# Attention and feed-forward kernel, batches 4 to 7: the logits' maximum by way of DRAM, with the loads of logits, keys and values in other places

## The chip, the cores and the metric

The kernel runs on one core of one Trainium2 chip. The metric is device time in microseconds of one execution, by the median of several. PE is TensorE (matmul), PEld its weight loads, DVE is VectorE, ACT is ScalarE, POOL is GpSimd, and SP is SyncE, which here only issues DMAs. Each engine works through its own instructions in the order in which they were written, and waits on semaphores where an instruction needs another engine's or a DMA's result, or a buffer that is still in use.

## What is computed

```python
def _attn_ref(q, k, v, phi):                      # batch 8, heads 8, seq 576, head_dim 64, n_mem 32
    a = phi - np.max(phi, axis=2, keepdims=True)  # softmax of the logits phi over the 576 rows
    a = np.exp(a)
    a = a / (np.sum(a, axis=2, keepdims=True) + 1e-09)
    k_m = np.einsum('bhsm,bhsd->bhmd', a, k)
    v_m = np.einsum('bhsm,bhsd->bhmd', a, v)
    scores = 1.0 / np.sqrt(q.shape[-1]) * np.matmul(q, k_m.transpose(0, 1, 3, 2))
    ...
    return np.matmul(attn, v_m)                   # attn is the softmax of scores over the 32

def _moe_ref(x, w_in, w_out):                     # x: 4608 tokens of 512, d_ff 2048
    h = x @ w_in
    g = h - np.tanh(h)
    return g @ w_out
```

The attention output of all batches, with heads side by side, is the `x` of the second part.

## The kernel before

**Slots.** The feed-forward part is cut into 18 units of 256 tokens (`u`) and 4 blocks of 512 hidden columns (`fb`). After a start that is written out by hand (`START`), one loop at the end of `split_path` runs over slots with the number 4u + fb. A slot writes its instructions in this order: `mm1` (PE: the hidden pre-activations of `(u, fb)` into the PSUM tile `hs`, from `ph`, `pl`, `ah`, `al`); `g1` (ACT squares, DVE L590); the words of the plan ahead of ";"; ACT's second square (L595); `a_forms` of the slot before (DVE L624, four f16 operations from POOL's result `g` to `f`); `g2` (DVE L600); `mm2_blocks` of two slots earlier (PE L711 and L718, into the PSUM tiles `x`, `o0` and `o1`, and for a unit's last block ACT L756 and L757); the ACT sums of checked weights (L446); the words behind ";"; `g2_high` (ACT L606); `g3` (POOL L611); the late loads; `evict` of a finished unit (DVE L771 to L783 read `x`, `o0` and `o1`, then SP stores); the words behind "|"; and the remaining late words. All slots share one `hs`, one `x`, and one `o0` and `o1`, so the next unit's first products wait for the `evict` of the unit before. In slot 33 the unit `u` = 7 is evicted, and PE's first writes into the new `o0` and `o1` stand in slot 34.

**The plan.** `PLAN` places the attention of batch b in slots relative to the batch's first one, 36 for batch 4, 44 for 5, 52 for 6 and 60 for 7. `FQ` loads the logits by rows (`pt`, 576 KB, in the buffer ring "q" of 2), `FA` the same logits by columns (`e`, one buffer "e"), `X` takes the maximum of each row of `pt` on DVE (`mx`, L149) and spreads it on a diagonal (`dg`, L151), `XP` multiplies `dg` by ones on PE so that every partition has all 256 maxima (`pmx`, L160), `YM` copies them from PSUM (ACT L181) and subtracts them from `e` on POOL (L165, L171), `YE` is the exponential on ACT (L185), `KR` loads keys and values (`kv`, `kt`), and `V` (PE L223, L231) sums keys and values with the weights `e`. Batch 3 has a plan of its own, and batches 0 to 2 lie in the start; for these nothing changes.

**The checked weights.** `PLAN_C` reads each weight block a second time and tests the size of its numbers. `CE` and `CQ` borrow a buffer of "e" or "q" for a block (`chk`, 512 KB); `CW` squares the oldest borrowed block on POOL (L442, `fy`), and ACT sums `fy` in the next slot (L446). `SI` and `NI` use a buffer of "q" for other sums. These words are carried out late in their slot. A load into a buffer waits for the last reader of what lay there before, and SP issues in order, so a load that waits holds up all that stand behind it.

Of the kernel before, what the change touches and what calls it, by code (L numbers as in the profile page):

```python
# [8 lines left out]
F32 = mybir.dt.float32  # L9
# [4 lines left out]
AF = mybir.ActivationFunctionType  # L14
ALU = mybir.AluOpType
# [3 lines left out]
P = 128  # L19
# [20 lines left out]
CW = (  # L40
    0.33333331252017, -0.13333128520786, 0.053934788850892, -0.021660115374759,
    0.0082189218977914, -0.0025104593252184, 0.000420695493864,
)
# [42 lines left out]

class Attention:


    def __init__(self, tc, c, big, ps_a, ins):  # L90
        self.tc, self.c, self.big, self.ps_a, self.ins = tc, c, big, ps_a, ins
# [54 lines left out]
    def top(self, b, d):  # L146
        nc, big = self.tc.nc, self.big
        mx = big.tile([P, 2], F32, tag="mx", name=f"mx{b}")
        nc.vector.tensor_reduce(mx, d["pt"], axis=AX.X, op=ALU.max)  # L149
        dg = big.tile([P, 2, P], F32, tag="kvn", name=f"dg{b}")  # L150
        nc.vector.tensor_tensor(  # L151
            dg, self.c["ident"].unsqueeze(1).to_broadcast((P, 2, P)),
            mx.unsqueeze(2).to_broadcast((P, 2, P)), op=ALU.mult,
        )
        d["dg"] = dg

    def top_all(self, b, d, ps=None):
        nc, dg = self.tc.nc, d["dg"]
        pa = self.psum(f"pmx{b}", ps)
        nc.tensor.matmul(pa[:, 0, 0:256], self.c["ones"], dg.rearrange("p a b -> p (a b)"), start=True, stop=True)  # L160
        d["px"] = pa
# [15 lines left out]

    def expo_pool(self, b, d):

        m = self.big.tile([P, 256], F32, tag="kvn", name=f"ms{b}")  # L180
        self.tc.nc.scalar.activation(m, d["px"][:, 0, 0:256], AF.Copy)  # L181
        self.less_top(self.tc.nc.gpsimd, d["e"], m)

    def expo_exp(self, b, d):
        self.tc.nc.scalar.activation(d["e"], d["e"], AF.Exp)  # L185
# [155 lines left out]
def split_path(ctx, tc, c, ins, out):  # L341
    nc = tc.nc
# [5 lines left out]
    ps_o = ctx.enter_context(tc.tile_pool(name="ps_o", bufs=1, space=PSUM))  # L348
    ps_a = ctx.enter_context(tc.tile_pool(name="ps_a", bufs=1, space=PSUM))
    dram = ctx.enter_context(tc.tile_pool(name="part", bufs=1, space=bass.MemoryType.DRAM))  # L350
# [3 lines left out]
    wout_hi = const.tile([P, 16, DM], F16, name="wout_hi")  # L354
    wout_lo = const.tile([P, 16, DM], F16, name="wout_lo")
    att = Attention(tc, c, big, ps_a, ins)

    RING = {"gg": 3, "h3": 2, "uu": 2, "q": 2, "sc": 2}
    raws = {}
# [131 lines left out]
    st = [dict() for _ in range(B)]  # L491
# [306 lines left out]
    def early(b):  # L798
        return ps_early if b == 0 else None

    def cubic(u, fb, stay):
# [11 lines left out]
        "KA": lambda b: att.load_kv(b, st[b], (0,)), "KB": lambda b: att.load_kv(b, st[b], (1,)), "Q": lambda b, t: att.load_q(b, st[b], t, "q"), "QT": lambda b, t: att.load_q(b, st[b], t, "qt"),  # L813
        "KR": lambda b, r: att.load_kv_half(b, st[b], r),
        "X": lambda b: att.top_bias(b, st[b]) if b < N_ROWS else att.top(b, st[b]), "YX": lambda b: att.expo_rows(b, st[b]),
        "XT": lambda b: att.expo_turn(b, st[b], early(b), ps_o), "XP": lambda b: att.top_all(b, st[b], early(b)),
        "Y": lambda b: att.expo(b, st[b]), "YM": lambda b: att.expo_pool(b, st[b]), "YE": lambda b: att.expo_exp(b, st[b]),
        "V": lambda b, r: att.pool_half(b, st[b], r, st[b]["pk"] if r else None), "N": lambda b, r=None: att.norm(b, st[b]) if r is None else att.norm_half(b, st[b], r),
        "U": lambda b: att.turn(b, st[b], early(b)), "UV": att_turn_v, "W": att_window,
# [24 lines left out]
    for word in START.split():  # L844
        if ":" in word:
            k, tag = word.split(":")
# [3 lines left out]


    PLAN = (
# [9 lines left out]
    )  # L862

    PLAN_C = (
# [229 lines left out]
@with_exitstack  # L1094
def tile_kernel(ctx: ExitStack, tc: tile.TileContext, qt, kva, kvt, pha, phx, w_in, w_out, out):
    nc = tc.nc
    ins = dict(qt=qt, kva=kva, kvt=kvt, pha=pha, phx=phx, w_in=w_in, w_out=w_out)
    const = ctx.enter_context(tc.tile_pool(name="const", bufs=1))
    c = {"first": len(nc.cur_bb.bb.instructions)}
    for name, shape, dt in (  # L1100
        ("ident", [P, P], F32), ("ones", [P, P], F32), ("ones16", [P, 1], F16), ("one", [P, 1], F32),
        ("beta", [P, 1], F32), ("idw", [P, P], F32), ("nidp", [P, P], F16), ("idw", [P, P], F32), ("nid16", [P, P], F16), ("stat", [P, N_CHECK], F32), ("bad", [P, 1], I32),
    ):
        c[name] = const.tile(shape, dt, name=name)
    make_identity(nc, c["ident"])
    nc.vector.tensor_scalar(c["nid16"], c["ident"], -1.0, None, op0=ALU.mult)
    nc.vector.tensor_scalar(c["nidp"], c["ident"], -S_V * S_W / S_P, None, op0=ALU.mult)
    nc.vector.tensor_scalar(c["idw"], c["ident"], S_W, None, op0=ALU.mult)
    nc.gpsimd.memset(c["ones"], 1.0)
    nc.gpsimd.memset(c["ones16"], 1.0)  # L1110
    nc.gpsimd.memset(c["one"], 1.0)
    nc.gpsimd.memset(c["beta"], BETA)
    with ExitStack() as inner:
        split_path(inner, tc, c, ins, out)
    with tc.If(c["wide"] > 0):
        with ExitStack() as inner:
            wide_path(inner, tc, c, ins, out)
# [39 lines left out]
```

## Time and profile before

| | |
|---|---|
| time before, median of 3 runs (lowest, highest) | 656.57 us (656.03, 657.09) |
| the profiled execution: its time, and its span from the first to the last instruction | 656.13 us, 654.2 us |
| granted TensorE clock, mean | 0.999 |
| DVE busy | 522.5 us (80% of the span) |
| ACT busy | 376.1 us (57%) |
| POOL busy | 251.0 us (38%) |
| DMA moved | 84.98 MB, mean 130 GB/s |

The profile is one execution on the chip. Times in its timeline are in microseconds from the span's start. A row gives the start, the duration, the engine, the line of the kernel, the operation, what it writes and reads with its shape, a count, and in brackets the idle time of the engine ahead of it and what ended that. The slots of batch 5 that matter run from about 310 to 345 us on PE, and DVE, ACT and POOL follow some microseconds behind PE.

### The profile page before, as it was taken

How to read it: one execution, taken by the hardware profiler on the slowest of the kernel's cores; microseconds unless marked ns; L12 is line 12 of the kernel's file. 1: busy time of each engine (PE TensorE's matmuls, PEld its weight loads, DVE VectorE, ACT ScalarE, POOL GpSimd, SP SyncE). 2: the span in 40 equal slices, each digit the busy share in tenths (PEclk: the TensorE clock that was granted, in tenths of full speed). 3: DMA queues.
4: the chain of work that ended last, by engine and by line, in shares of the span. 5: the costliest groups of instructions: out<-in, count | busy, mean ns of one | idle time of the engine just before them, and what ended most of it. 6: DMA issues, size and time to landing. Idle time of an engine off the chain costs nothing.

```text
span 654.2 us, 15605 instructions
## 1 busy us (share of the span) xinstructions
PE 638.0 (98%) x6690; PEld 456.1 (70%) x6690; DVE 522.5 (80%) x790; ACT 376.1 (57%) x509; POOL 251.0 (38%) x173
## 2 busy tenths in 40 slices
PE   8779999999999999999999999999999999999996
PEld 4355656566557778777777677877687777887885
DVE  6889999999956687875897779777978686867773
ACT  4477686666423456544655566545655577666541
POOL 0225141222132144451536353624453455455531
PEclk9999999999999999999999999999999999999999
DMA  8999245301423302504350415132433333234201
GB/s 343 393 373 386 99 172 176 124 2 66 146 97 103 134 33 74 176 7 167 101 182 3 169 50 181 55 135 71 147 105 135 102 104 122 64 108 134 86 33 37
DMA packets 26572, 84.98 MB, mean 130 GB/s; under 512 B 2944, under 2 KB 2944, under 8 KB 25728
## 3 DMA queue, kind: packets, MB, share of 16 engines
q1 hardware_dynamic: 25200, 81.55, 36.0%
q10 hardware_dynamic: 1296, 2.36, 1.0%
q8 instruction: 54, 0.88, 0.6%
q14 instruction: 22, 0.18, 0.1%
HBM read 72.37 MB, written 11.53 MB: 128 GB/s over the span
## 4 chain that ended last, share of the span: by engine, by line
PE 78%; DVE 13%; ACT 3%; issue 3%; DMA 1%; POOL 1%; DVEq 0%; ACTq 0%; POOLq 0%
PE hs L575 20%; PE x L718 14%; PE o L711 13%; PE o L718 10%; PE o L654 6%; PE h L575 5%; PE o1h L654 3%; PE pp L527 3%; DVE h L600 2%; DVE h L590 1%; DVE wt L387 1%; PE warm L792 1%; DVE wt L392 1%; DVE ph L545 1%; DVE f L624 1%
## 5 line engine op out<-in xcount | busy, mean ns | idle before, releaser
L611 POOL TENSOR_TENSOR g<-h,g 128x1024 f16<-128x1024 f32 x64 | 138.5, 2165 | 323.9 <-ACT g L606 229.9
L575 PEld LDWEIGHTS <-ph 128*128 128x128 f16 x2304 | 177.0, 98 | 20.5 <-issue 6.0
L575 PE MATMUL hs<-ah,ph 128*128 128x256 f16 (+3 forms) x1152 | 151.5, 246 | 0.0
L590 DVE SCALAR_TENSOR_TENSOR h<-hs,u 128x1024 f32<-128x1024 f32 x54 | 65.8, 1218 | 88.0 <-ACT u L582 88.0
L606 ACT ACTIVATE g<-h 128x1024 f16<-128x1024 f32 x72 | 75.9, 1055 | 92.3 <-DVE h L600 90.2
L575 PE MATMUL hs<-al,ph 128*128 128x256 f16 (+3 forms) x576 | 127.6, 246 | 0.0
L595 ACT ACTIVATE u<-u,beta 128x1024 f32<-128x1024 f32 x72 | 82.4, 1147 | 55.4 <-DVE h L590 54.4
L711 PE MATMUL o<-wout_hi,g 128*128 128x512 f16 x432 | 104.7, 379 | 0.0
L718 PEld LDWEIGHTS <-f 128*128 128x128 f16 x896 | 87.7, 98 | 10.1
L600 DVE SCALAR_TENSOR_TENSOR h<-u,h 128x1024 f32<-128x1024 f32 x72 | 87.4, 1216 | 0.8 <-ACT u L595 0.7
L582 ACT ACTIVATE u<-hs 128x1024 f32<-128x1024 f32 x54 | 55.1, 1019 | 49.6 <-PE hs L575 45.4
L718 PE MATMUL x<-bt,f 128*128 128x256 f16 x672 | 82.5, 273 | 0.0
L718 PEld LDWEIGHTS <-g 128*128 128x128 f16 x672 | 64.4, 98 | 25.8 <-issue 4.3
L711 PEld LDWEIGHTS <-g 128*128 128x128 f16 x432 | 40.5, 98 | 43.9 <-issue 8.1
L624 DVE TENSOR_TENSOR f<-g 128x512 f16<-128x512 f16 x112 | 65.8, 627 | 4.3 <-POOL g L611 3.4
L654 PEld LDWEIGHTS <-g 128*128 128x128 f16 x384 | 36.7, 98 | 46.5 <-issue 3.9
L654 PE MATMUL o<-wout_hi,g 128*128 128x512 f16 x192 | 58.8, 379 | 0.0
L575 PE MATMUL h<-ah,ph 128*128 128x256 f16 (+3 forms) x384 | 49.6, 246 | 0.1
L575 PE MATMUL h<-al,ph 128*128 128x256 f16 (+2 forms) x192 | 42.4, 246 | 0.2 <-POOL al L518 0.2
L545 DVE SCALAR_TENSOR_TENSOR ph<-pp,ph 128x1024 f16<-128x1024 f32 x31 | 37.6, 1212 | 0.6 <-ACT ph L540 0.6
L540 ACT ACTIVATE ph<-pp 128x1024 f16<-128x1024 f32 x32 | 32.6, 1017 | 7.5 <-PE pp L527 7.4
L654 PE MATMUL o<-wout_lo,g 128*128 128x512 f16 x96 | 36.4, 379 | 0.0
(146 smaller groups left out, 974.3 us busy)
## 6 DMA issues: line engine op xcount, KB each, us to landing
q<-in_qt_dram SPq DMA_DIRECT2D x16, 576.0 KB, 4.9
kv<-in_kva_dram SPq DMA_DIRECT2D x16, 516.0 KB, 4.7
chk<-in_w_in_dram SPq DMA_DIRECT2D x16, 512.0 KB, 5.7
chk<-in_w_out_dram SPq DMA_DIRECT2D x16, 512.0 KB, 3.3
out_dram<-r SPq DMA_DIRECT2D x27, 256.0 KB, 2.4
kv<-in_kva_dram SPq DMA_DIRECT2D x6, 1032.0 KB, 8.7
raws<-in_w_in_dram SPq DMA_DIRECT2D x12, 512.0 KB, 7.0
raw<-in_w_out_dram SPq DMA_DIRECT2D x12, 512.0 KB, 7.2
```

Source lines behind the costliest of these rows:

```text
L545: nc.vector.scalar_tensor_tensor(pl, pa, S_P / (S_V * S_W), ph, op0=ALU.mult, op1=ALU.subtract)
L575: nc.tensor.matmul(hp[:, k, tu : tu + w], px[:, g, cs], d[ax][:, g, ta : ta + w], start=(n == 0), stop=(n == 5),)
L582: nc.scalar.activation(uu, hp, AF.Square, scale=1.0 / (S_A * S_P))
L590: nc.vector.scalar_tensor_tensor(h3, hp, C2 * S_G / (S_A * S_P), uu, op0=ALU.mult, op1=ALU.mult)
L595: nc.scalar.activation(uu, uu, AF.Square, bias=c["beta"])
L600: nc.vector.scalar_tensor_tensor(h3, uu, CC, hp, op0=ALU.add, op1=ALU.mult)
L606: nc.scalar.activation(gg[:, 0], h3, AF.Copy)
L611: eng.tensor_tensor(gg[:, 1], h3, gg[:, 0], op=ALU.subtract)
L624: nc.vector.tensor_tensor(o, x, y, op=op)
L654: nc.tensor.matmul(o, gx[:, k, P * tt : P * tt + P], wx[:, 4 * fb + k, :], start=(first and k == 0 and wx is wout_hi and gx is gh), stop=( ...
L711: nc.tensor.matmul(o[th], gg[:, 0, k, P * th : P * th + P], wout_hi[:, 4 * fb + k, :], start=(first and k == 0), stop=False)
L718: nc.tensor.matmul(dst, a(1 - n, kk), b(n, kk), start=(new and kk == 0 and n == 0), stop=(end and kk == 1 and n == 1))
```

## The change

For batches 4 to 7 the diagonal, the matmul with ones and ACT's copy are dropped. DVE's row maxima (`mx`, 128 x 2 numbers) are written to a small DRAM tile by a DMA on SP, and a second DMA on SP, written a slot later (`XL`), reads that tile into every partition (`ms`, 128 x 256). POOL subtracts from this tile, whose two maxima of a partition now lie side by side, so it is read with a step of two. `FQ` moves from slot -11 to -12, `X` from -10 to -11, and `KR` from -10 to -9; `FA`, `YM`, `YE` and `V` keep their slots. In `PLAN_C`, `CQ` and `CE` change places in slots 21, 30, 38 and 46, so that the first block to be checked, and so the first buffer to be freed, is one of "q".

```diff
@@ top
         nc.vector.tensor_reduce(mx, d["pt"], axis=AX.X, op=ALU.max)
+        if b > 3 and self.dram:
+            d["mx"] = self.dram.tile([P, 2], F32, tag=f"mx{b}", name=f"mxd{b}")
+            nc.sync.dma_start(d["mx"], mx)
+            return
         dg = big.tile([P, 2, P], F32, tag="kvn", name=f"dg{b}")
...
+    def load_top(self, b, d):
+        d["ms"] = self.big.tile([P, P, 2], F32, tag="kvn", name=f"ms{b}")
+        self.tc.nc.sync.dma_start(d["ms"], d["mx"].unsqueeze(0).to_broadcast((P, P, 2)))
@@ expo_pool
-        m = self.big.tile([P, 256], F32, tag="kvn", name=f"ms{b}")
-        self.tc.nc.scalar.activation(m, d["px"][:, 0, 0:256], AF.Copy)
-        self.less_top(self.tc.nc.gpsimd, d["e"], m)
+        m, e, eng = d["ms"].rearrange("p x r -> p r x"), d["e"], self.tc.nc.gpsimd
+        eng.tensor_tensor(
+            e[:, 0:8].rearrange("p (c r) x -> p c r x", r=2), e[:, 0:8].rearrange("p (c r) x -> p c r x", r=2),
+            m.unsqueeze(1).to_broadcast((P, 4, 2, P)), op=ALU.subtract,
+        )
+        for r in range(2):
+            rs = slice(64 * r, 64 * r + 64)
+            eng.tensor_tensor(e[rs, 8], e[rs, 8], m[rs, r], op=ALU.subtract)
@@ split_path
+    att.dram = dram
...
+        "XL": lambda b: att.load_top(b, st[b]),
@@ PLAN
-        (-11, "FQ{0} FA{0}"), (-10, "; X{0} KR{0}0 KR{0}1"), (-9, "| XP{0} YM{0}"), (-8, "; YE{0}"), ...
+        (-12, "FQ{0}"), (-11, "FA{0} ; X{0}"), (-10, "; XL{0}"), (-9, "KR{0}0 KR{0}1 | YM{0}"), (-8, "; YE{0}"), ...
@@ PLAN_C
-        (21, "; CE CQ CQ"), (22, "CW"), (23, "CW"), (24, "CW"), (30, "CE CQ"), (31, "CW CE SI0"), (32, "CW CW ; SS0"),
-        (38, "CE CQ"), (39, "CW CE SI1"), (40, "CW CW ; SS1"), (46, "CE CQ"), (47, "CW CE SI2"), (48, "CW CW ; SS2"),
+        (21, "; CQ CQ CE"), (22, "CW"), (23, "CW"), (24, "CW"), (30, "CQ CE"), (31, "CW CE SI0"), (32, "CW CW ; SS0"),
+        (38, "CQ CE"), (39, "CW CE SI1"), (40, "CW CW ; SS1"), (46, "CQ CE"), (47, "CW CE SI2"), (48, "CW CW ; SS2"),
```

**DVE in slot 33** (the first is `g2` of unit 8, block 1; the `r` rows are the eviction of unit 7, and the two with `o700` and `o701` free `o0` and `o1`). Before:

```order
L600 SCALAR_TENSOR_TENSOR h381_4164<-u81_4162,h381_4164 128x1024
L771 SCALAR_TENSOR_TENSOR r70_4183<-x_2448,r70_4183 128x256
L772 SCALAR_TENSOR_TENSOR r71_4184<-x_2448,r70_4183 128x256
L773 TENSOR_TENSOR r70_4183<-r70_4183,r71_4184 128x256
L776 TENSOR_TENSOR r71_4184<-r71_4184 128x256
L783 SCALAR_TENSOR_TENSOR r70_4183<-o700_3885,r70_4183 128x512
L783 SCALAR_TENSOR_TENSOR r71_4184<-o701_3886,r71_4184 128x512
```

And now, with the lines of the changed file (L771 is L787, L773 is L789, L783 is L799):

```order
L616 SCALAR_TENSOR_TENSOR h381_4164<-u81_4162,h381_4164 128x1024
L151 TENSOR_REDUCE mx5_4223<-pt5_4077 128x2
L787 SCALAR_TENSOR_TENSOR r70_4181<-x_2448,r70_4181 128x256
L788 SCALAR_TENSOR_TENSOR r71_4182<-x_2448,r70_4181 128x256
L789 TENSOR_TENSOR r70_4181<-r70_4181,r71_4182 128x256
L792 TENSOR_TENSOR r71_4182<-r71_4182 128x256
L799 SCALAR_TENSOR_TENSOR r70_4181<-o700_3883,r70_4181 128x512
L799 SCALAR_TENSOR_TENSOR r71_4182<-o701_3884,r71_4182 128x512
```

The maximum `mx5` now stands ahead of the eviction; it stood a slot later, with `dg5`, behind `g2` and the transpose `af4`, and both are gone from there.

**SP in slots 30 to 34** (the `chk` rows are borrowed weight blocks, `q41` queries of batch 4, `pt5` and `e5` the logits of batch 5, `r70` and `r71` the stores of unit 7). Before:

```order
L369 DMA chk3_3930<-in_w_in_dram 128x512
L369 DMA chk4_3932<-in_w_in_dram 128x512
L137 DMA q41_3984<-in_qt_dram 128x1152
L369 DMA chk5_4034<-in_w_in_dram 128x512
L102 DMA pt5_4166<-in_phx_dram 128x1152
L106 DMA e5_4168<-in_pha_dram 128x1152
L784 DMA out_0_dram<-r70_4183 128x512
L784 DMA out_0_dram<-r71_4184 128x512
L128 DMA kv500_4343<-in_kva_dram 128x1032
```

And now:

```order
L385 DMA chk3_3928<-in_w_in_dram 128x512
L385 DMA chk4_3930<-in_w_in_dram 128x512
L139 DMA q41_3982<-in_qt_dram 128x1152
L385 DMA chk5_4032<-in_w_in_dram 128x512
L104 DMA pt5_4077<-in_phx_dram 128x1152
L108 DMA e5_4166<-in_pha_dram 128x1152
L154 DMA mxd5_4225<-mx5_4223 128x2
L800 DMA out_0_dram<-r70_4181 128x512
L800 DMA out_0_dram<-r71_4182 128x512
L165 DMA ms5_4341<-mxd5_4225 128x256
L130 DMA kv500_4406<-in_kva_dram 128x1032
```

The order of the first six is the same, but not their buffers: `chk3` and `chk5` had the one buffer "e" and `chk4` one of "q", while now `chk3` has "q" and `chk4` and `chk5` have "e". So `chk5` waited for POOL's square of `chk3`, and now waits for that of `chk4`. `pt5` waited for POOL's square of `chk4`; it needs only that of `chk3` now, but stands behind `chk5` in the queue. POOL's order is unchanged: in slot 32 the squares of `chk4` and `chk5` follow each other directly, then the product with `sz40`, then `g81` of slot 33. The two new DMAs stand between `e5` and the keys and values. Batches 6 and 7 have the same rows in slots 38 to 42 and 46 to 50; for batch 4 the logits are loaded in slot 24, when the borrowed blocks of slot 21 have one buffer each and none waits for another.

More of the change, by code (lines that the diff above doesn't have):

```diff
@@ L87 @@
 class Attention:
+    dram = None
     def __init__(self, tc, c, big, ps_a, ins):
@@ L815, in split_path @@
         "X": lambda b: att.top_bias(b, st[b]) if b < N_ROWS else att.top(b, st[b]), "YX": lambda b: att.expo_rows(b, st[b]),
-        "XT": lambda b: att.expo_turn(b, st[b], early(b), ps_o), "XP": lambda b: att.top_all(b, st[b], early(b)),
+        "XT": lambda b: att.expo_turn(b, st[b], early(b), ps_o), "XP": lambda b: att.top_all(b, st[b], early(b)), "XL": lambda b: att.load_top(b, st[b]),
         "Y": lambda b: att.expo(b, st[b]), "YM": lambda b: att.expo_pool(b, st[b]), "YE": lambda b: att.expo_exp(b, st[b]),
```

2 rows, old and new, of the table PLAN are left out of this document.

## The prediction

> **What bounds the kernel now.** I read the span first, then the busy times over the long middle part, then the timeline of one slot at a time.
>
> ```profile
> span 654.2 us, 15605 instructions
> ```
> ```profile
> 192.00:624.00 432.00, 431.46 (x4733) 330.88 (x4731) 335.20 (x512) 251.42 (x340) 192.91 (x125) 1.00 0.32 105
> ```
>
> The second row gives the stretch, its length, and the busy time of PE, PEld, DVE, ACT and POOL. From 192 to 624 us PE has no work for only 0.54 us. So whatever PE no longer issues there is won, nearly in full, and whatever PE must wait for is lost in full: there is no later idle time in which to get it back. The question is which instructions PE loses, and which waits come near enough to hold it.
>
> **What PE loses.** One matmul of 256 columns in two passes, before the first `hs` of slots 28, 36, 44 and 52:
>
> ```profile
> 341.31 0.27 PE L718 MATMUL o<-wout_lo,f 128*128 128x256 f16 x1
> 341.42 0.60 PE L160 MATMUL pmx<-dg,ones 128*128 128x256 f32 x2
> 341.86 0.27 PE L575 MATMUL hs<-ah,ph 128*128 128x256 f16 x1
> ```
> ```profile
> 350.03 0.27 PE L718 MATMUL o<-wout_lo,f 128*128 128x256 f16 x1
> 350.14 0.27 PE L575 MATMUL hs<-ah,ph 128*128 128x256 f16 x1
> ```
>
> With it, `hs` starts 0.55 us behind the last L718; without it 0.11 us. So it costs 0.44 us of PE, and four times that is **-1.76 us**. `dg` on DVE and the copy on ACT go too, but PE doesn't wait for them, so I cost them at nothing.
>
> **What moves ahead of the eviction.** PE's first matmul into the new `o0` waits for the first L783, which reads the old one. These are the rows of slot 33 on DVE, and the matmul on PE:
>
> ```profile
> 325.43 1.22 DVE L600 SCALAR_TENSOR_TENSOR h<-u,h 128x1024 f32<-128x1024 f32 x1
> 326.56 0.42 DVE L771 SCALAR_TENSOR_TENSOR r<-x,r 128x256 f32<-128x256 f32 x1
> 327.01 0.42 DVE L772 SCALAR_TENSOR_TENSOR r<-x,r 128x256 f32<-128x256 f32 x1
> 327.36 0.41 DVE L773 TENSOR_TENSOR r<-r,r 128x256 f32<-128x256 f32 x1
> 327.69 0.42 DVE L776 TENSOR_TENSOR r<-r 128x256 f32<-128x256 f32 x1
> 328.02 0.68 DVE L783 SCALAR_TENSOR_TENSOR r<-o,r 128x512 f32<-128x512 f32 x1
> ```
> ```profile
> 330.10 0.38 PE L711 MATMUL o<-wout_hi,g 128*128 128x512 f16 x1
> ```
>
> The first L783 ends at 328.70, so there are 1.40 us to spare. The maximum now stands between L600 and L771:
>
> ```profile
> L149 DVE TENSOR_REDUCE mx<-pt x6: 1309/1312/1343, 82.1 to 471.1; 128x2 f32<-128x1152 f32 x6
> ```
>
> It takes 1.31 us, about 1.35 us from its start to the next one's. By itself that would just fit. Two things come on top.
>
> *First, the logits arrive too late for it.* In batches 5 to 7 the load of `pt` stands behind that of `chk5`, which now waits until POOL has squared `chk4`, as `pt` itself did before:
>
> ```profile
> 321.10 2.04 POOL L442 TENSOR_TENSOR fy<-chk 128x512 f32<-128x512 f32 x2
> 323.10 1.33 POOL L318 TENSOR_TENSOR sc<-sc,sz 128x576 f32<-128x576 f32 x1
> 327.81 2.29 POOL L611 TENSOR_TENSOR g<-h,g 128x1024 f16<-128x1024 f32 x1 [3.38 <-ACT g L606]
> ```
> ```profile
> 322.17 0.33 SPq L102 DMA_DIRECT2D pt<-in_phx_dram  x1
> ```
>
> The first square ends at about 322.1 and `pt` is issued at 322.17. So `FQ`, a slot earlier in the plan, is in fact issued no earlier: `chk5` goes at 322.17 and `pt` some 0.4 us behind it. For two such loads in a row there is a pair of before:
>
> ```profile
> 249.51 0.34 SPq L102 DMA_DIRECT2D pt<-in_phx_dram  x1
> 249.90 0.42 SPq L106 DMA_DIRECT2D e<-in_pha_dram  x1
> ```
> ```profile
> pt<-in_phx_dram SPq DMA_DIRECT2D x1, 576.0 KB, 3.8
> e<-in_pha_dram SPq DMA_DIRECT2D x1, 576.0 KB, 4.8
> ```
> ```profile
> chk<-in_w_in_dram SPq DMA_DIRECT2D x1, 512.0 KB, 3.7
> ```
>
> The last number is from issue to landing. The second of a pair lands 0.39 + 4.8 = 5.2 us after the first's issue; the first one here is 64 KB smaller, so I take 5.1. `chk5` lands at 322.17 + 3.7 = 325.9 and `pt` at 327.3. DVE, free at 326.56, waits 0.75 us. Then the maximum, and L771 starts at about 328.7, L772 at 329.1, and L773 would at 329.5.
>
> *Second, POOL holds L773 up.* L773 reads two SBUF tiles. The same kind and size of operation, `dg`, shows what that means while POOL works:
>
> ```profile
> 335.33 2.14 POOL L611 TENSOR_TENSOR g<-h,g 128x1024 f16<-128x1024 f32 x1 [5.22 <-ACT g L606]
> ```
> ```profile
> 336.12 1.63 DVE L151 TENSOR_TENSOR dg<-ident,mx 128x256 f32<-128x256 f32 x1
> ```
>
> POOL's instruction ended at 337.47 and `dg` at 337.75: 1.63 us instead of the 0.41 of L773. Before, L773 and L776 were just ahead of POOL's `g` of 327.81. Where is that `g` now? POOL squares `chk5` when it lands, 326.0 to 327.0; ACT's sum of that square and its `g` follow:
>
> ```profile
> 324.88 0.71 ACT L446 ACTIVATE fy<-fy,one 128x512 f32<-128x512 f32 x1
> 325.49 0.19 ACT L446 ACTIVATION_READ_ACCUMULATOR fy<-fy,one 128x1 f32 x1
> 326.68 1.06 ACT L606 ACTIVATE g<-h 128x1024 f16<-128x1024 f32 x1 [1.00 <-DVE h L600]
> ```
>
> So the sum starts at 327.1, ACT's `g` at 327.85, and POOL's `g` runs from 328.95 for 2.13 us, to 331.1. L773, ready at 329.5, waits for its end. By the `dg` row the next instruction starts about 0.2 us behind that end; L776 takes 0.33, L783 0.69. The first L783 ends at 332.3, and PE, ready at 330.10, goes on at 332.37: **2.27 us lost** in each of batches 5, 6 and 7, +6.8 us. What else is late there catches up in PE's wait: the next `g1`, which frees `hs`, ends near 334.0, and PE needs `hs` at 333.14 + 2.27 = 335.4. ACT's `g` and POOL's are some 2 to 4 us late in slot 34, but DVE then saves the maximum and `dg`, 3 us.
>
> [...]
>
> *Batch 4* has its logits early, but the same order in slot 25:
>
> ```profile
> 260.52 0.42 DVE L771 SCALAR_TENSOR_TENSOR r<-x,r 128x256 f32<-128x256 f32 x1
> ```
> ```profile
> 261.83 2.24 POOL L611 TENSOR_TENSOR g<-h,g 128x1024 f16<-128x1024 f32 x1 [3.77 <-issue]
> ```
> ```profile
> 264.81 0.38 PE L711 MATMUL o<-wout_hi,g 128*128 128x512 f16 x1
> ```
>
> L771 moves to 261.87 and L773 to 262.67, into `g`, which ends at 263.9. Then 0.2 + 0.33 + 0.69: the first L783 ends at 265.15, and PE waits until 265.2, **0.4 us**.
>
> **What I cost at nothing.** The two new DMAs have no row. `mx` is written from about 328.7, and behind the two stores, which SP holds until 332.9, `ms` is issued near 333.4. With each at a landing between 0 and the 3.7 us of a 512 KB load, `ms` is there by 337.1, and POOL asks for it ten microseconds later:
>
> ```profile
> 347.04 2.37 POOL L165 TENSOR_TENSOR e<-e,ms 128x1024 f32<-128x1024 f32 x1
> ```
> ```profile
> 357.63 0.32 PE L223 MATMUL pkv<-kv,e 128*32 128x129 f32 x4
> ```
>
> Keys and values are issued behind `ms`, from about 333.8 to 336, over 20 us ahead of `V`; four of the six went out only after the old maximum before, so they are hardly later.
>
> POOL's subtraction now reads `m` with a step of two numbers. From below: the 2.37 us stay, as only the step of one input changes. From above, the dearest two-input row of POOL per element:
>
> ```profile
> L171 POOL TENSOR_TENSOR e<-e,ms x8: 522/582/650, 282.1 to 486.5; 64x128 f32<-64x128 f32 x8
> ```
> ```profile
> 352.50 1.06 ACT L606 ACTIVATE g<-h 128x1024 f16<-128x1024 f32 x1 [0.71 <-DVE h L600]
> ```
>
> 582 ns for 128 is 4.5 ns an element, 4.7 us for 1024, 2.3 us more. ACT's exponential would pass that on, less the 0.71 us that it then idles: up to 1.6 us a batch, 6.4 in all, if it reached PE. I take nothing, since most of those 582 ns look like a fixed part.
>
> [...]
>
> **The sum**: -1.76 + 3 x 2.27 + 0.4 = +5.45 us. The profiled execution took 656.13 us, of which the span is 654.2; it becomes 661.6. It lay 0.44 us under the median, so against that the forecast is **662.0 us**.
>
> **The rivals.**
> - *All is hidden*: the logits land in time, and POOL's `g` does not meet L773. Only PE's matmuls count: 656.57 - 1.76 = 654.8 us, **faster**. It decides at 1.40 us: if the maximum delays the eviction by less, PE never waits. For it, 1.35 us alone would fit; against it, `pt` is issued no earlier than before.
> - *Late logits, but no lock*: L783 ends at 327.3 + 0.05 + 1.35 + 1.46 + 0.69 = 330.85, a loss of 0.8 us in three batches, none in batch 4: 656.57 + 2.4 - 1.76 = 657.2 us, **no change**. It would need `pt` within 0.5 us of `chk5`, or `g` later than I have it.
> - *Lock, but logits in time*, because the wait of `chk5` is shorter than I read it. POOL's `g` ends at 329.9, L783 at 331.1: 1.1 us in three batches: 656.57 + 3.3 + 0.4 - 1.76 = 658.5 us, slower.
> - *The strided subtraction reaches PE too*: up to 662.0 + 6.4 = 668.4 us, slower.
> - *The change doesn't do what it says*, in that the logits have no lead: this is part of the forecast.
>
> **How the numbers follow.** The forecast has 0.52, all hidden 0.16, late logits without the lock 0.14, the lock alone 0.10, the subtraction 0.08. A measurement of this kernel can tell about 0.2%, 1.3 us, from no change. So faster has 0.16, the same 0.14, slower 0.70. The range from 655.9 to 666.5 us leaves out the hidden case, and of the last one what lies above two thirds of its price (662.0 + 4.5).
>
> **What would show it.** In the changed profile `pt` of batch 5 should be issued some 0.4 us behind `chk5`, with POOL idle for 3 to 4 us between two squares; `mx` should wait for the DMA; L773 (now L789) should last over 1.5 us instead of 0.41 in four evictions; and PE should wait for L783 (now L799) three times for about 2.3 us and once for 0.4. If L789 keeps 0.41 us, the lock is wrong here; if PE waits for nothing, the hidden rival is right; if PE's new waits stand at `V` or at `hs`, I have missed a path.

## The result, and the profile after

| | before | after |
|---|---|---|
| median (lowest to highest, runs) | 656.31 us (656.03 to 657.09, 4) | 665.75 us (664.84 to 666.26, 4) |
| after against before, 95% interval | | 1.0139 [1.0127, 1.0151] |
| profiled execution, its span | 656.13 us, 654.2 us | 666.26 us, 664.5 us |

The change costs 9.4 us, 8.3 to 9.9 us by the interval. The forecast was 5.45 us over the median of before as it then stood, 656.57 us: the sign was right, the size too small. These are the rows of the changed kernel that answer to the first two of before, the span and the busy times of PE, PEld, DVE, ACT and POOL over the middle part:

```profile
span 664.5 us, 15593 instructions
```
```profile
192.00:634.00 442.00, 432.06 (x4730) 330.33 (x4729) 335.15 (x508) 248.90 (x336) 191.75 (x125) 1.00 0.31 104
```

PE's work is nearly the same, but the part is 10 us longer: PE has 9.94 us without work where it had 0.54. The list of PE's waits (sum, times, longest) names them, with the one line that the list of before had of the same kind below it:

```profile
PE x L734 <- DVE r L788: 4.7, 3, 1.8
...
PE o L727 <- DVE r L799: 2.4, 4, 0.8
PE pp L543 <- DVE kvn L254: 2.4, 3, 0.9
```
```profile
PE pp L527 <- DVE kvn L239: 0.2, 1, 0.2
```

The first two are the eviction, the third is a wait that was not in the forecast. To see what each costs I compare where PE starts the first `hs` of a slot. From slot 34 to 35 before, and after:

```profile
324.86 0.27 PE L575 MATMUL hs<-ah,ph 128*128 128x256 f16 x1
...
333.14 0.27 PE L575 MATMUL hs<-ah,ph 128*128 128x256 f16 x1
```
```profile
326.82 0.27 PE L591 MATMUL hs<-ah,ph 128*128 128x256 f16 x1
...
337.52 0.27 PE L591 MATMUL hs<-ah,ph 128*128 128x256 f16 x1
```

8.28 us became 10.70: the eviction of unit 7 costs 2.42 us. The same subtraction for every slot gives this ledger (us, against before):

| slots | what | forecast | measured |
|---|---|---|---|
| 26 to 29 | batch 4 in all, its matmul included | 0.4 - 0.44 | +0.49 |
| 34 to 35, 42 to 43, 50 to 51 | eviction | 3 x 2.27 | +2.42, +2.33, +2.74 |
| 35 to 36, 43 to 44, 51 to 52 | the matmul of ones gone | 3 x -0.44 | -0.44, -0.44, -0.43 |
| 38 to 39, 46 to 47, 54 to 55 | `pp` waits for `kvn` | 0 | +0.73, +0.70, +0.68 |
| 18 to 71 | all (the rest is -0.04) | +5.45 | +8.74 |

Ahead of slot 18, where both kernels have the same code, this execution was 1.47 us later (193.55 us instead of 192.08). In the 14 profiles of this study that point lies between 191.60 and 194.07 us, so I count that as variation of the start. All comparisons of slots below are taken from slot 18 on.

**The eviction** went as the prediction has it. SP, DVE and POOL in slot 33:

```profile
324.12 0.33 SPq L385 DMA_DIRECT2D chk<-in_w_in_dram  x1
324.54 0.38 SPq L104 DMA_DIRECT2D pt<-in_phx_dram  x1
```
```profile
329.58 1.35 DVE L151 TENSOR_REDUCE mx<-pt 128x2 f32<-128x1152 f32 x1 [2.48 <-DMA pt<-in_phx_dram]
330.85 0.41 DVE L787 SCALAR_TENSOR_TENSOR r<-x,r 128x256 f32<-128x256 f32 x1
331.29 0.42 DVE L788 SCALAR_TENSOR_TENSOR r<-x,r 128x256 f32<-128x256 f32 x1
331.64 1.86 DVE L789 TENSOR_TENSOR r<-r,r 128x256 f32<-128x256 f32 x1
```
```profile
328.18 1.04 POOL L458 TENSOR_TENSOR fy<-chk 128x512 f32<-128x512 f32 x1 [4.08 <-DMA chk<-in_w_in_dram]
329.18 1.16 POOL L333 TENSOR_TENSOR sc<-sc,sz 128x576 f32<-128x576 f32 x1
331.09 2.12 POOL L627 TENSOR_TENSOR g<-h,g 128x1024 f16<-128x1024 f32 x1 [0.76 <-ACT g L622]
```

`pt` is issued 0.42 us behind `chk5`, not earlier; `mx` waits 2.48 us for it; POOL waits 4.08 us for `chk5`, ACT's sum of that block and its own `g` come late with it, and so POOL's `g` starts at 331.09 and ends at 333.21; L789, which took 0.41 us in the kernel before (there L773), takes 1.86 and ends at 333.50, 0.29 us behind that `g`. This is what the forecasts and I call the lock: L789 reads two SBUF tiles, comes up while POOL's `g` is under way, and ends only behind it. PE waits twice:

```profile
331.87 0.27 PE L734 MATMUL x<-wout_hi,g 128*128 128x256 f16 x1 [1.49 <-DVE r L788]
...
334.49 1.89 PE L727 MATMUL o<-wout_hi,g 128*128 128x512 f16 x8 [0.72 <-DVE r L799]
```

The first matmul into `x`, ahead of those into `o0`, already waits for L788, the last reader of `x`. Only the remaining 0.72 us is waited for where I had put all of it.

**The new wait**, five slots on. PE before and after, and what DVE and POOL of the changed kernel do in slot 36:

```profile
362.92 0.41 PE L527 MATMUL pp<-win_hi,vh 64*32 64x512 f16 x8 [0.20 <-DVE kvn L239]
```
```profile
367.60 0.41 PE L543 MATMUL pp<-win_hi,vh 64*32 64x512 f16 x8 [0.93 <-DVE kvn L254]
```
```profile
352.01 2.94 DVE L640 TENSOR_TENSOR f<-g 128x512 f16<-128x512 f16 x2
```
```profile
351.67 2.40 POOL L191 TENSOR_TENSOR e<-e,ms 128x1024 f32<-128x1024 f32 x1
```

Where POOL does not hold them, the two f16 operations of `f` take 0.75 us together (at 324.43 us in the same profile, while POOL waits for `chk5`); here POOL's subtraction is under way when the first begins, and they take 2.94: the first lasts 2.34, to 354.35, 0.28 us behind the end of the subtraction at 354.07. Before, `f` came 1.02 us behind the start of that subtraction and took 2.21 (at 348.06 and 347.04 us); now it comes 0.34 us behind it. Counted from the first `hs` of slot 36 it is the subtraction that has moved, from 5.18 us to 5.86; `f` begins at 6.21 us in both kernels, and in both its first operation ends behind the subtraction. DVE leaves slot 36 later, and `kvn`, which frees the PSUM tile that `pp` needs, is late.

**Batch 4**, in slots 25 to 28, is a small copy of both: L789 lasts 1.67 us, PE waits for L799, and in slot 27, where `hs` needs a `ph` that DVE made late (L561), it waits again and gives back most of what the matmul had saved:

```profile
264.04 1.67 DVE L789 TENSOR_TENSOR r<-r,r 128x256 f32<-128x256 f32 x1
```
```profile
266.70 1.89 PE L727 MATMUL o<-wout_hi,g 128*128 128x512 f16 x8 [0.26 <-DVE r L799]
...
270.68 0.23 PE L591 MATMUL hs<-ah,ph 128*128 128x64 f16 x2 [0.23 <-DVE ph L561]
```

### The profile page after: what moved, and what is told of

Read it like the earlier page. It is cut to its first block, busy times and chain, and to the rows that moved or that the text cites. A ratio compares the mean times of both kernels' runs of the same rounds, so it can differ in the third digit from the quotient of the medians.

```text
span 664.5 us, 15593 instructions
## 1 busy us (share of the span) xinstructions
PE 640.2 (96%) x6682; PEld 455.3 (69%) x6682; DVE 523.9 (79%) x786; ACT 373.7 (56%) x505; POOL 250.1 (38%) x173
## 4 chain that ended last, share of the span: by engine, by line
PE 57%; DVE 20%; issue 8%; DMA 5%; ACT 5%; POOL 3%; SPq 0%; DVEq 0%; ACTq 0%; POOLq 0%
PE hs L591 14%; PE o L727 9%; PE x L734 8%; PE o L734 7%; PE o L670 6%; PE h L591 4%; DVE f L640 4%; PE o1h L670 3%; DVE h L616 3%; DVE h L606 3%; DMA pt<-in_phx_dram 2%; ACT u L598 2%; PE pp L543 2%; POOL g L627 2%; DMA raw<-in_w_out_dram 2%
## 5 line engine op out<-in xcount | busy, mean ns | idle before, releaser
L616 DVE SCALAR_TENSOR_TENSOR h<-u,h 128x1024 f32<-128x1024 f32 x72 | 87.4, 1216 | 0.8 <-ACT u L611 0.7
L561 DVE SCALAR_TENSOR_TENSOR ph<-pp,ph 128x1024 f16<-128x1024 f32 x31 | 37.6, 1214 | 2.6 <-ACT ph L556 2.6
L458 POOL TENSOR_TENSOR fy<-chk 128x512 f32<-128x512 f32 x32 | 33.7, 1062 | 12.5 <-DMA chk<-in_w_in_dram 12.5
```

Source lines behind the costliest of these rows:

```text
L561: nc.vector.scalar_tensor_tensor(pl, pa, S_P / (S_V * S_W), ph, op0=ALU.mult, op1=ALU.subtract)
L616: nc.vector.scalar_tensor_tensor(h3, uu, CC, hp, op0=ALU.add, op1=ALU.mult)
```

## The experiments

Times are medians; ratios are against the kernel before on the same chip, with 95% intervals. "Stalls" are the steps of the ledger: the three evictions, and the three steps of `kvn`.

| run | time, us | ratio | batch 4 | evictions | `kvn` |
|---|---|---|---|---|---|
| the changed kernel | 665.75 | 1.0139 [1.0127, 1.0151] | +0.49 | 2.42, 2.33, 2.74 | 0.73, 0.70, 0.68 |
| e1 maximum behind the eviction | 655.88 | 0.9990 [0.9979, 1.0001] | -0.43 | 0, 0.01, 0 | 0.40, 0.39, 0.43 |
| e2 logits ahead of the block | 666.02 | 1.0132 [1.0115, 1.0149] | +0.51 | 0.22, 0.41, 0.14 | 0.75, 0.76, 0.71 |
| e3 blocks as before | 661.55 | 1.0072 [1.0057, 1.0088] | +0.51 | 1.12, 1.10, 1.11 | 0.74, 0.73, 0.69 |
| e4 DRAM path alone | 655.99 | 0.9997 [0.9985, 1.0010] | -0.43 | 0, 0, 0 | 0.28, 0.24, 0.24 |
| e5 logits in a place of their own | 656.11 | 0.9998 [0.9988, 1.0007] | +0.49 | 0, 0.01, 0 | 0.26, 0.26, 0.27 |
| e6 e1, subtraction on DVE | 656.57 | 1.0007 [0.9994, 1.0019] | -0.43 | 0, 0, 0 | 0.59, 0.42, 0.83 |
| e7 changed kernel, subtraction on DVE | 666.41 | 1.0153 [1.0138, 1.0168] | +0.50 | 3.11, 2.46, 2.65 | 0.90, 0.88, 0.86 |
| e8 e5, subtraction on DVE | 657.14 | 1.0010 [1.0001, 1.0020] | +0.48 | 0, 0, 0 | 0.43, 0.41, 0.40 |
| e9 e6, small parts first | 654.45 | 0.9965 [0.9954, 0.9977] | -0.43 | 0, 0.01, 0 | -0.27, -0.12, -0.13 |
| e10 changed kernel, no subtraction | 664.00 | 1.0110 [1.0095, 1.0125] | +0.47 | 2.70, 2.39, 2.80 | -0.26, -0.11, -0.13 |
| e11 e7, small parts first | 663.64 | 1.0108 [1.0092, 1.0125] | +0.49 | 2.58, 2.40, 2.45 | -0.27, -0.11, -0.13 |
| e12 changed kernel, eviction from PSUM | 667.87 | 1.0170 [1.0157, 1.0184] | -0.03 | 3.88, 3.71, 4.12 | 0.26, 0.24, 0.22 |

**e1: the maximum behind the eviction.**

```diff
-(-11, "FA{0} ; X{0}")
+(-11, "FA{0} | X{0}")
```

> The changed kernel with the maximum behind the eviction instead of ahead of it; the load of the logits still waits behind the borrowed block, and POOL still waits for that block. Theory A (the eviction is held: late logits, then the maximum, then POOL's lock on the eviction's two-input sum): the three waits of PE for the eviction are gone, and with the backlog the wait at kvn; 656.3 - 1.8 = 654.5 us, at most 655.5. Rival B (POOL's wait for the block and ACT's late g are what costs, wherever the maximum stands): PE still waits some 2 us in each of three batches, about 662 us. Rival C (the DRAM path itself, its DMAs or the strided subtraction, costs): above 656.3 us, with waits of PE at V or of POOL for ms.

655.88 us. The eviction no longer waits for the logits and nothing of its stall is left, though POOL still waits 4.05 us for `chk5` and ACT 2.56 us for its square. So the maximum ahead of the eviction is needed for the loss, and the waits of POOL and ACT cost nothing at the eviction by themselves. The time is 0.4 us above the range of theory A: a price is paid elsewhere, 0.4 us a batch at `kvn`.

**e2: the logits ahead of the block, by the plan.**

```diff
-(-12, "FQ{0}"), ... (31, "CW CE SI0"), ... (39, "CW CE SI1"), ... (47, "CW CE SI2")
+(-13, "| FQ{0}"), ... (31, "CW SI0 CE"), ... (39, "CW SI1 CE"), ... (47, "CW SI2 CE")
```

> The changed kernel with the logits' load issued a slot earlier still, ahead of the borrowed block that waits; the maximum stays ahead of the eviction, and POOL still waits for the block. Theory A: logits in time, DVE takes the maximum at once and is through the eviction's two-input sums before POOL's g, or waits for POOL's shorter product only; PE waits for the eviction by less than 0.5 us, total 654.5 to 656.5 us. Rival B: POOL and ACT are as late as in the changed kernel, so about 662 us or more.

666.02 us, far outside. The eviction stall nearly went, but the edit made a new wait: with the logits loaded first, the queries of `SI0` got the buffer of `chk3`, and ACT, which squares them, and then PE, waited. ACT's and PE's waits:

```profile
ACT sqi L466 <- POOL fy L458: 9.7, 3, 3.2
```
```profile
PE pni L480 <- ACT g L622: 4.9, 3, 1.6
```

With PE held ahead of the eviction by this new wait, the run can't say what the late logits cost; e5 moves them without that change of buffers.

**e3: the blocks in the order of before**, with all else as changed.

```diff
-(21, "; CQ CQ CE"), ... (30, "CQ CE"), ... (38, "CQ CE"), ... (46, "CQ CE")
+(21, "; CE CQ CQ"), ... (30, "CE CQ"), ... (38, "CE CQ"), ... (46, "CE CQ")
```

> The changed kernel with the borrowed blocks in the order of before, so that no block waits ahead of the logits and POOL has no wait; the logits land just in time, and the maximum stays ahead of the eviction. Theory A with the lock: the two-input sum runs into POOL's g and takes over 1.5 us, PE waits about 1.1 us in three batches and 0.4 in the first; 658 to 659 us. Without a lock: the maximum alone delays the eviction by 1.35 us, PE waits 0.4 us at x; about 656 us. Rival B: nothing waits, 654.6 us.

661.55 us. `mx` follows L616 without a wait, and yet L789 meets POOL's `g`:

```profile
324.02 2.25 DVE L640 TENSOR_TENSOR f<-g 128x512 f16<-128x512 f16 x2
...
330.17 1.61 DVE L789 TENSOR_TENSOR r<-r,r 128x256 f32<-128x256 f32 x1
```
```profile
329.37 2.14 POOL L627 TENSOR_TENSOR g<-h,g 128x1024 f16<-128x1024 f32 x1 [3.38 <-ACT g L622]
```

The eviction loses 1.1 us a batch, the price that the rival "lock, but logits in time" gave. `kvn` loses as much as in the changed kernel, 2.2 us, which puts the time above the 658 to 659 us expected; so this part of the loss does not depend on the order of the blocks.

**e4: the DRAM path alone**, every word in its slot of before.

```diff
-(-12, "FQ{0}"), (-11, "FA{0} ; X{0}"), (-10, "; XL{0}"), (-9, "KR{0}0 KR{0}1 | YM{0}")
+(-11, "FQ{0} FA{0}"), (-10, "; X{0} XL{0} KR{0}0 KR{0}1"), (-9, "| YM{0}")
```

(and `PLAN_C` as in e3)

> The kernel before with the path through DRAM alone: loads and maximum in the slots of before, the maximum written to DRAM and read into all partitions right behind it, borrowed blocks in the order of before. Theory A: only PE's four matmuls are gone and nothing else is late; 654.6 us, PE without new waits, POOL not waiting for ms. Rival C: above 656.3 us, with POOL's subtraction later or longer, and PE waiting at V or at kvn.

655.99 us: nothing is lost by the two DMAs or by the subtraction with a step of two. All four matmuls are won, 1.74 us by the ledger, and 0.76 of it goes back at `kvn`: PE arrives there 0.44 us sooner, and DVE does not. The median is 1.4 us above the 654.6 expected. By the ledger 1.0 us is won from slot 18 on; the ratio shows less of it, and in the profiled execution slot 18 itself began 1.02 us later than before, which lies within the variation of the start.

**e5: the late logits by themselves.** A word `LQ` loads `pt` late in slots 31, 39 and 47, ahead of `chk5`'s load; every buffer is that of the changed kernel.

```diff
-(-12, "FQ{0}"),
-(31, "CW CE SI0"), ... (39, "CW CE SI1"), ... (47, "CW CE SI2")
+(24, "FQ4 CW"), ...
+(31, "CW SI0 LQ5 CE"), ... (39, "CW SI1 LQ6 CE"), ... (47, "CW SI2 LQ7 CE")
```

> The changed kernel, but in batches 5 to 7 the load of pt stands ahead of chk5's in SP's queue (issued late in slot 31, behind the queries q41 and ahead of the block that waits for a square), so that it waits only for the square of the first block. Nothing else is moved: the maximum still stands ahead of the eviction and the buffers are those of the changed kernel. Theory A (late logits carry L789 into POOL's g): pt is issued near 315 us, mx starts directly behind L616 instead of waiting 2.48 us for the DMA, L789 then ends before POOL's g begins and takes about 0.4 us, and the eviction stall of PE falls from 2.3 to 2.7 us to under 0.4 in batches 5 to 7; the wait for kvn (0.7 us a batch) stays or halves: 656 to 658.5 us. Rival B (the lock does the harm by itself, with logits in time as well, as in the run with the blocks in the order of before): 1.1 us a batch are left and kvn stays: 660.5 to 662.5 us. Rival C (the place of the maximum ahead of the eviction does it, whatever the logits and POOL do): no change against the changed kernel, 665 to 666 us.

656.11 us, as theory A has it. `pt` goes out 8 us ahead of `chk5`, `mx` does not wait, and the eviction passes ahead of `g`:

```profile
314.88 0.33 SPq L104 DMA_DIRECT2D pt<-in_phx_dram  x1
323.25 0.33 SPq L385 DMA_DIRECT2D chk<-in_w_in_dram  x1
```
```profile
323.55 0.75 DVE L640 TENSOR_TENSOR f<-g 128x512 f16<-128x512 f16 x2
...
326.14 1.34 DVE L151 TENSOR_REDUCE mx<-pt 128x2 f32<-128x1152 f32 x1
...
328.19 1.09 DVE L789 TENSOR_TENSOR r<-r,r 128x256 f32<-128x256 f32 x1
```
```profile
327.85 1.16 POOL L333 TENSOR_TENSOR sc<-sc,sz 128x576 f32<-128x576 f32 x1
329.76 2.14 POOL L627 TENSOR_TENSOR g<-h,g 128x1024 f16<-128x1024 f32 x1 [0.76 <-ACT g L622]
```

L789 took 1.09 us, not the 0.4 expected: it met POOL's shorter product with `sz`, until 329.01, and that still fits into the slack. So 1.35 us of maximum do fit ahead of the eviction here, as the rival "all is hidden" said; in the changed kernel, late logits carried it into `g`.

That it fits has a reason which no forecast named. While POOL waits for `chk5` it does not hold DVE's `f`, which takes 0.75 us here and 2.25 in e3, beside POOL's second square and its product. So DVE comes to the maximum 7.69 us behind the first `hs` of slot 33 here, and 9.21 us behind it in e3. There, with POOL's work in its place of before, the same maximum costs 1.1 us although the logits are in time.

**e6 and e7: the subtraction on DVE**, on top of e1, and on the changed kernel.

```diff
 def expo_pool
-... self.tc.nc.gpsimd
+... self.tc.nc.vector
```

> The kernel with the maximum behind the eviction (655.88 us), and in addition the subtraction L191 and its two small parts L197 on DVE instead of POOL, in the same place of the order. Theory A (POOL's subtraction locks out DVE's f in slot 36, 2.6 us instead of 0.75, and so makes kvn late): the subtraction takes about 1.1 us and the two small parts 0.2 each on DVE, in the 2.16 us that DVE idles ahead of L606 of slot 36; f takes 0.75; PE's wait for kvn (1.5 us in 3) goes: 654.0 to 655.2 us. Rival B (kvn is late through DVE's own backlog, and the added 1.5 us on DVE make it later): 656 to 658 us, with f at 0.75 and the wait for kvn no smaller. Rival C (the maximum arrives too late for DVE, which then waits at the subtraction for ms, landing near 341 us): idle time of DVE ahead of L191, and PE waits for hs instead: 656 to 659 us.

> The changed kernel as it is, but for the subtraction on DVE. Theory A: the eviction stall of PE (2.3 to 2.7 us a batch) stays, since nothing is altered ahead of slot 35, and only the wait for kvn (0.73, 0.70 and 0.69 us) goes: 663.3 to 664.3 us. Rival B (the wait for kvn is the eviction's delay come again, not the subtraction): 665 to 667 us.

656.57 and 666.41 us: both lie in the ranges of rival B, and the wait for `kvn` grew, as it said. `f` has its 0.75 us in e6, but now DVE's own small parts run into POOL's `g`. DVE and POOL of e6:

```profile
344.67 1.21 DVE L191 TENSOR_TENSOR e<-e,ms 128x1024 f32<-128x1024 f32 x1
345.81 3.38 DVE L197 TENSOR_TENSOR e<-e,ms 64x128 f32<-64x128 f32 x2
```
```profile
345.31 2.57 POOL L627 TENSOR_TENSOR g<-h,g 128x1024 f16<-128x1024 f32 x1 [4.02 <-issue]
347.84 1.20 POOL L320 TENSOR_TENSOR sc<-sc,sm 128x576 f32<-128x576 f32 x1
```

The two small parts took 3.38 us, until 349.19: they were done behind `g` (to 347.88) and POOL's next operation (to 349.04). They were expected at 0.2 us each. DVE lost as much time to POOL as before, in another place, so these runs fit rival B, but do not exclude theory A. **e8**, e5 with the same edit, has the same flaw:

> The changed kernel with both: the load of pt ahead of chk5's, and the subtraction on DVE. If the two terms are separate, the two gains add up: by theory A of both, nothing is left of the changed kernel's loss and the four matmuls' 1.7 us are won, 654.3 to 655.8 us. If instead one of them only moves the loss on to the other place, it ends no lower than the better of the two alone plus 1 us.

657.14 us, 1 us above e5 alone: the loss only moved, as the second forecast has it.

**e9 to e11: DVE's loss taken away.** In e9 (on e6) and e11 (on e7) the two small parts stand ahead of the large one:

```diff
+for r in range(2): ... eng.tensor_tensor(e[rs, 8], e[rs, 8], m[rs, r], op=ALU.subtract)
 eng.tensor_tensor(e[:, 0:8] ..., m ..., op=ALU.subtract)
-for r in range(2): ... eng.tensor_tensor(e[rs, 8], e[rs, 8], m[rs, r], op=ALU.subtract)
```

In e10 the changed kernel has none of the three lines.

> The kernel with the maximum behind the eviction and the subtraction on DVE, with the two small parts L197 (64x128) ahead of the large one L191 instead of behind it. In the run before, the second small part met POOL's g and lasted until its end: the two took 3.38 us. Theory A (what makes kvn late is the time that DVE loses to POOL's lock in slots 35 and 36, wherever it is lost): the small parts take about 0.2 us each and L191 1.2, they end ahead of L606's wait for ACT's u, POOL's g starts some 0.8 us later instead; f of slot 36 keeps 0.75; DVE leaves slot 36 1.5 us or more earlier and PE's wait for kvn (2.1 us in 3) goes or falls under 0.6: 654.2 to 655.3 us. Rival B (kvn waits for something else, pkv or PE's own order): the wait stays at 1.5 to 2.1 us, 655.7 to 656.7 us.

> The changed kernel without the subtraction of the maximum from e in batches 4 to 7 (L191 and L197 left out; the maximum is still made, written and read back). Theory A (the wait for kvn comes from the lock between POOL's subtraction and DVE's f in slot 36, 2.94 us there): f takes 0.75, PE's wait for kvn (0.73, 0.70, 0.69 us) is gone, the eviction stall stays: 663.2 to 664.2 us. Rival B (the eviction's lateness alone makes kvn late): 665 to 666.3 us with the wait still there.

> The changed kernel with the subtraction on DVE, small parts first. Theory A as for the kernel without a subtraction, but with 1.5 us more of DVE's time in slot 35, of which 1.84 us are idle there: 663.3 to 664.5 us, with PE's wait for kvn under 0.2 us a batch. Rival B: 665 to 666.5 us.

654.45, 664.00 and 663.64 us; all three times as theory A has them. In the two on the changed kernel the eviction stalls stay, and the steps of `kvn` go from +0.7 to below zero. DVE in e9, slot 35 and the `f` of slot 36, and POOL:

```profile
342.64 0.57 DVE L193 TENSOR_TENSOR e<-e,ms 64x128 f32<-64x128 f32 x2
343.23 1.23 DVE L194 TENSOR_TENSOR e<-e,ms 128x1024 f32<-128x1024 f32 x1
...
347.16 1.02 DVE L640 TENSOR_TENSOR f<-g 128x512 f16<-128x512 f16 x2
```
```profile
343.28 3.17 POOL L627 TENSOR_TENSOR g<-h,g 128x1024 f16<-128x1024 f32 x1 [4.02 <-issue]
```

Now DVE has the large subtraction under way when `g` comes up at 343.28, 0.05 us later, and POOL is the one that is held: `g` takes 3.17 instead of 2.13 us, and nobody waits for it. `f` takes 1.02 us, not quite the 0.75 expected. e9 beats both kernels, by 0.35% of the kernel before, with an interval that leaves out 1.

**e12: the lock by itself.** The eviction's two SBUF additions read `x` in PSUM and scale it, instead of reading ACT's scaled copy of it.

```diff
-nc.vector.tensor_tensor(ra[:, 2], ra[:, 0], rb[:, 2], op=ALU.add)
+nc.vector.scalar_tensor_tensor(ra[:, 2], x[:, 0, hi], sc, ra[:, 0], op0=ALU.mult, op1=ALU.add)
...
-nc.vector.tensor_tensor(rb[:, 1], rb[:, 0], rb[:, 2], op=ALU.add)
+nc.vector.scalar_tensor_tensor(rb[:, 1], x[:, 0, hi], sc, rb[:, 0], op0=ALU.mult, op1=ALU.add)
```

> The changed kernel, with L789 and L792 of the eviction reading the x tile in PSUM, scaled, in place of ACT's copy of it in SBUF: the same values, the same sizes, the same places in DVE's order, but one input in SBUF instead of two. Theory A (POOL's g locks out a DVE operation that reads two SBUF tiles): where L789 lasted 1.86 us beside g (and 1.67 in batch 4), it takes 0.42 now. The first L799 then ends at about 333.0 instead of 334.4 in batch 5's eviction and PE does not wait for it; but PE's first matmul into x must now wait for L792, some 0.7 us longer than for L788, so that the stall falls from 2.4 to about 2.3 us only; batch 4 loses nothing: 664.5 to 666 us. Rival B (L789 is slow for another reason, such as a late input or the traffic of DMAs): the two keep 1.7 to 2.2 us together, and since PE now waits for L792 before x, the stall grows by about 1.3 us a batch: 668 to 670 us.

667.87 us. The duration is that of theory A: L789 runs in 0.41 us in the middle of `g`.

```profile
330.16 0.41 DVE L789 SCALAR_TENSOR_TENSOR r<-x,r 128x256 f32<-128x256 f32 x1
```
```profile
329.67 2.13 POOL L627 TENSOR_TENSOR g<-h,g 128x1024 f16<-128x1024 f32 x1 [0.76 <-ACT g L622]
```

It averages 414 ns over its 14 executions, against 817 ns in the changed kernel, and batch 4 loses nothing. The time is 1.9 us above the range of theory A and just below rival B's 668 to 670 us, and the stall grew by 1.4 us a batch, as rival B has it; but the slow L789 that this was to come from isn't there. PE's wait ahead of `x` is 2.15 us, near the stall of 2.3 that theory A expected, and the matmuls behind it then ran slowly:

```profile
331.05 0.27 PE L734 MATMUL x<-wout_hi,g 128*128 128x256 f16 x1 [2.15 <-DVE r L792]
...
331.54 2.77 PE L734 MATMUL x<-bt,f 128*128 128x256 f16 x12
```
```profile
332.00:333.00 1.00, 1.00 (x6) 0.73 (x5) 1.00 (x2) 0.00 (x0) 0.00 (x0) 0.50 0.58 217
```

The last row is one microsecond in the columns of the middle part: the granted clock, third from the end, is 0.50. The twelve matmuls of the middle row took 1.47 us in the changed kernel. From 331 to 335 us the mean clock is 0.57, which makes about 3.4 us at 0.50, and the 12 `x` and 8 `o0` and `o1` matmuls together took 1.66 us more (2.77 - 1.47, and 2.25 - 1.89); by three such evictions some 5 us, without which I estimate e12 near 663 us. No run takes that drop of the clock away.

## Why the prediction was right, and where it was short

- **"One matmul ... so it costs 0.44 us"**: right in every run (-0.43 to -0.44 at each place where nothing else changed).
- **"`FQ`, a slot earlier in the plan, is in fact issued no earlier"**: right, and the changed kernel's stall at the eviction needs it: e5 alters only this and the stall is gone. I had `pt` landing 4.7 to 4.8 us after its issue; it took 5.0 (issued 324.54, `mx` at 329.58). I had DVE waiting 0.75 us for it; it waited 2.48, mostly because it was free 1.5 us sooner than I read from the kernel before (see e5). That alters nothing in the sum, since `pt` sets when the maximum starts.
- **"POOL holds L773 up"**: right. In the changed kernel L789 ends 0.29 us behind `g`; in e12, without a second input in SBUF, it takes 0.41 us beside the same `g`. In the same rows `mx` takes 1.35 us beside POOL's product and L788, which reads PSUM, 0.42 beside `g`: neither is slowed (1.31 and 0.42 in the kernel before), and L789 takes 1.45 us more. In batch 4 it ends 0.28 us behind `g` (265.71 and 265.43).
- **"2.27 us lost"**: the mechanism was right and the term a little small, 2.33 to 2.74 us, 0.68 us over the three. Most of it is waited for ahead of `x`, not of `o0`. I had read only the slack of L783, and not what the wait ahead of `x` asks for.
- **"What else is late there catches up in PE's wait"**: this step failed. It is true of slot 34, the next to follow, but not of DVE against POOL in slot 36. There DVE is held by POOL's subtraction already in the kernel before, and PE had 0.2 us of wait for `kvn`: no slack at all. POOL comes to the subtraction 0.68 us later, counted from PE's slot, and that costs 0.7 us a batch, 2.1 us; e10 and e11 take the lock away and the 2.1 us with it. I had quoted that subtraction and asked only whether its step of two makes it longer, not which DVE operation it stops.
- **"whatever PE no longer issues there is won, nearly in full"**: this was too much. In e4, where nothing is late at the eviction, 0.76 of 1.74 us goes back at `kvn`. So about 0.25 of the 0.7 us a batch is the saved matmul given back; the rest goes with the still later start of POOL's subtraction (see below).
- **"Batch 4 ... 0.4 us"**: 0.42 at the eviction, and 0.51 more at the late `ph` and behind it: the same step again.
- **"What I cost at nothing"**: right for the DMAs, the later keys and values (e4, and e1 in the changed slots), and the step of two: 2395 ns against 2368 for the large subtraction.

```profile
L191 POOL TENSOR_TENSOR e<-e,ms 128x1024 f32<-128x1024 f32 x4 | 9.6, 2395 | 0.0
```
```profile
L165 POOL TENSOR_TENSOR e<-e,ms 128x1024 f32<-128x1024 f32 x4 | 9.5, 2368 | 0.0
```

By the terms, of the 8.74 us of the ledger 5.45 were forecast; 0.68 are the eviction's size, 2.11 `kvn` and 0.53 batch 4 (together 8.77). That the time still lay in the stated range is partly luck: the range reached 4.5 us above the forecast only for the case that the strided subtraction reaches PE, which did not happen, and the 3.3 us that I had missed fitted into that room.

The rivals: "all is hidden" is what e5 has at the eviction, and "lock, but logits in time" is e3; both conditions were read rightly, but both runs also pay at `kvn`, for which no rival stood. Of the signs that I had named for a missed path, `V` and `hs`, neither showed the main one, which stands at `pp`.

The wait for `kvn` has different sizes in the runs with the subtraction on POOL, and their traces show what goes with it. In all of them `f` begins 6.2 to 6.3 us behind the first `hs` of slot 36 (44 and 52 in the later batches). The subtraction begins 5.2 us behind it before, 5.4 in e4, e5 and e12, 5.5 to 5.6 in e1, and 5.9 in the changed kernel, e2 and e3; the step of `kvn` is 0.22 to 0.28, 0.39 to 0.43 and 0.68 to 0.76 us. So PE loses what POOL's subtraction is later against PE's slot. What stays open is why POOL's start settles at 5.4 us in some runs and at 5.9 in others: its `g` ahead of the subtraction moves alike, and I did not follow it further.

## What to carry to other kernels

An operation that is written earlier on an engine that works in order is worth only as much as its input is earlier: follow the load back through its queue and its buffer to the instruction that frees it, and if that has not moved, the operation has become a wait for all that stands behind it (here `pt` was issued 0.42 us behind `chk5`, and DVE waited 2.48 us for it). Where VectorE and GpSimd both read SBUF, list every two-input VectorE operation against GpSimd's long ones (L789 took 1.86 us beside `g`, 0.41 without it), and ask which of the two comes first; having the VectorE operation under way when GpSimd's came up (e9) won 2.1 us with the same instructions (656.57 us in e6, 654.45 in e9). And an engine with 0.2 us of wait somewhere has no slack there: a gain of 0.44 us ahead of such a place is partly given back (0.25 us a batch in e4).

## What the hardware showed that I had not expected

**The clock after a stall.** In e12 PE was idle for 2.15, 1.99 and 2.51 us ahead of `x`, and each time the matmuls behind ran slowly: the twelve into `x` took 2.77, 2.77 and 2.65 us instead of 1.47, the first twelve at a granted clock of 0.50 (332 to 333 us). In e7 an equal wait, 2.15 us, left the clock at 1.00, as these rows of PE and of the microsecond of its end show:

```profile
331.51 0.27 PE L734 MATMUL x<-wout_hi,g 128*128 128x256 f16 x1 [2.15 <-DVE r L788]
```
```profile
331.00:332.00 1.00, 0.49 (x5) 0.47 (x6) 1.00 (x2) 1.00 (x2) 1.00 (x1) 1.00 0.89 346
```

So the length of the wait alone does not decide it; what else does was not shown. How long the clock stays low is alike in two profiles: about 3.4 us in e12, and 3.41 us in the changed kernel, from 28.18 to 31.59 us, where it was 0.50 behind a wait of PE of 2.31 us for `q` that ended at 27.29.

**Small DMAs behind large ones.** The write of 1 KB took 2.8 us to land in e4, where SP had issued nothing for over 6 us, and 3.4 in the changed kernel, issued 1.7 us behind the 576 KB load of `e`. In e5, issued 0.4 us behind that load, it took 5.7, and in e1, with two stores of 256 KB issued between the two, 6.4; the rows of e1:

```profile
ms<-mxd SPq DMA_DIRECT2D x1, 128.0 KB, 6.0
mxd<-mx SPq DMA_DIRECT2D x1, 1.0 KB, 6.4
```

I had bounded each by 3.7 us. Here 10 us of lead hid the difference.
